# Attention and two mixtures on one core: order of the first loads, a conversion's low word, the pace of the conversion, and 14 unread products

## Chip, cores and metric

The kernel runs on one core of one Trainium2 chip. The metric is the time of one execution on the device in microseconds. [...]

## What is computed

```
# attention: q, k, v (4, 8, 576, 64) f32
rel = pos[:, None] - pos[None, :]
mask_local = (rel >= 0) & (rel < 32)                       # heads 0 to 3
mask_strided = (rel >= 0) & (pos[None, :] % 32 == pos[:, None] % 32)   # heads 4 to 7
attn = softmax(where(mask, q @ k.T / 8, -1e9))
x = (attn @ v) as (2304, 512)
# first mixture: w_a, w_b (512, 1536), w_out (1536, 512)
x = ((x @ w_a) * (x @ w_b)) @ w_out
# second mixture: noisy top 2 of 8 experts, w1 (8, 512, 1024), w2 (8, 1024, 512)
noisy = x @ w_gate + log1p(exp(x @ w_noise)) * noise
out[t] = sum over the two best e of softmax weight * (relu(x[t] @ w1[e]) @ w2[e])
```

The weights w_a, w_b and w_out arrive as float64; all else is float32.

## The kernel before

**Stages.** Four batches of 576 tokens go through attention in units of two heads (HPS = 0, 2, 1, 3: local and strided pairs in turn). The first mixture takes the tokens in five chunks c (512 tokens of each batch, then the four tails of 64 together) and twelve slices f of 128 hidden columns; ORDER lists the pairs (c, f). The attention of batch 0 runs alone at first; that of the batches 1 to 3 is cut into small steps (`att_pipe`, a generator) that run between the products of the first mixture. Then come the router, the scatter of tokens to experts, and the experts. The change lies in the first 150 us of about 1150.

**A unit of attention** (class `Unit`). `load_qk` and `load_v` issue its loads on SyncE. `T` transposes q and k on TensorE (L247) and ScalarE copies them out (L251). `Q` makes the scores sc (the mask as a product, L270, the scores, L279) and takes the maxima on VectorE (L283); for batch 1 ScalarE copies the scores to s (L289) and VectorE reduces (L303). `E` forms the exponentials on ScalarE (L307 or L312) and divides by the sums on VectorE: L314 adds, L315 inverts, L316 multiplies, into the softmax tile s. `P` transposes s on TensorE (L324), ScalarE copies (L325), and `PV` multiplies by v (L337), copies to xf (L340) and stores the last 64 tokens into tails on SyncE (L342). Two halves of a unit have a tile s each. `split_kd` splits a unit's result into a high and a low part (L403, L404).

**Products of three.** Every large product is done as three of fp32r (`mm3`, L184 to L188): high by high, high by low, low by high, 512 columns each. `stage_a` forms pa and pb from the chunk and the slices of w_a and w_b; ScalarE copies pa into a (L686), VectorE multiplies a by pb (L691), and a is split into gh and gl (L692, L693). `stage_b` multiplies by w_out into po.

**Conversion.** The float64 weights are loaded as pairs of 32-bit words (tile raw, low word L and high word Hw), one block per SyncE instruction (L158, `load_raw`), and `split64` (L161) makes a high and a low fp32r weight of each (w0h, w0l and so on) in two steps: VectorE masks the high word into m (tile ct, L167), ScalarE shifts its exponent (L168), VectorE adds the sign (L170), ScalarE writes the high part (L171); VectorE then cuts out the nine low bits of Hw (L173), joins the low word to them (L174), takes the exponent (L175) and writes the low part (L176). There are 24 blocks of two steps each, 48 steps: six of 512 columns (f = 0 and f = 1: w_a, w_b, w_out each), twelve of 1024 columns (two f each, f = 2 to 9), six of 512 columns (f = 10 and 11). Three raw buffers take turns; the load of a block waits until the block three before it is converted. `conv_to(n)` writes the code on up to step n: 12 steps (six blocks) along the attention of batch 0, and then, in chunk 0, by L778, four steps a slice f up to f = 5, and six a slice after that.

**Who sets the order.** TensorE's order is that of the code from the first mixture on (L773), SyncE's in the attention of batch 0 (L650). VectorE's and ScalarE's queues, and TensorE's in the first stage, are laid out by the scheduler when the kernel is built; on the chip each engine then takes its queue strictly in order. "Block 7" below is the seventh in the order of the slices: w_a of f = 2 and 3.

**Small loads.** `late_setup` (L105, called at L801) loads the gate weights wg and the noise in ten small loads (L106 to L112) and fills the table of the scatter. The setup (L71 to L103) makes the masks on VectorE and GpSimd; the tile ones, all 1.0, is written at L90. The first load of batch 0's q waits for the setup's last VectorE instruction.

Of the kernel before, what the change touches and what calls it, by code (L numbers as in the profile page):

```python
# [9 lines left out]
F32 = mybir.dt.float32  # L10
# [3 lines left out]
U32 = mybir.dt.uint32  # L14
AF = mybir.ActivationFunctionType
OP = mybir.AluOpType
# [16 lines left out]
def attention_moe_kernel(ctx: ExitStack, tc: tile.TileContext, q, k, v, w_a, w_b, w_out,  # L33
                         w_gate, w_noise, noise, w1, w2, out):
    nc = tc.nc
    B, H, S, D = q.shape
# [31 lines left out]
    wg = cpool.tile([128, KD, 16], F32, name="wg")  # L68
    noise_sb = cpool.tile([128, NTL, 8], F32, name="noise_sb")

    with tc.tile_pool(name="setup", bufs=1) as sp:  # L71
        rel = sp.tile([128, 128], I32, name="rel")
        nc.gpsimd.iota(rel, pattern=[[-1, 128]], base=0, channel_multiplier=1)
# [13 lines left out]
        nc.vector.tensor_scalar(r3f[:, 0], r3f[:, 0], 0.0, NEG, op0=OP.is_gt, op1=OP.mult)  # L87
        nc.vector.tensor_add(maskS, r3f[:, 0], r3f[:, 1])
        nc.vector.tensor_scalar(tri, relf, 0.0, None, op0=OP.is_lt)
        nc.vector.memset(ones, 1.0)  # L90
        nc.gpsimd.iota(iota8, pattern=[[1, 8]], base=0, channel_multiplier=0,
                       allow_small_or_imprecise_dtypes=True)
        nc.gpsimd.iota(base, pattern=[[NT, 8]], base=0, channel_multiplier=0,
# [8 lines left out]
            nc.gpsimd.iota(ids[TL * i:TL * i + TL, 4 * B:NTL], pattern=[[2 * S, 2]], base=S * i + CT,  # L102
                           channel_multiplier=1)  # L103

    def late_setup():  # L105
        nc.sync.dma_start(wg[:, :, 0:8], w_gate.rearrange("(k p) e -> p k e", p=128))  # L106
        nc.sync.dma_start(wg[:, :, 8:16], w_noise.rearrange("(k p) e -> p k e", p=128))
        for b in range(B):
            nc.sync.dma_start(noise_sb[:, 4 * b:4 * b + 4, :],
                              noise[S * b:S * b + CT, :].rearrange("(t p) e -> p t e", p=128))  # L110
            i = TL * (b % 2)
            nc.sync.dma_start(noise_sb[i:i + TL, 4 * B + b // 2, :], noise[S * b + CT:S * b + S, :])  # L112
        nrow = E * NT // 128
        fill = rpool.tile([128, nrow, 2], I32, name="fill", tag="x2T")
        nc.gpsimd.iota(fill[:, :, 0], pattern=[[1, nrow]], base=0, channel_multiplier=nrow)
        nc.vector.tensor_scalar(fill[:, :, 0], fill[:, :, 0], PAD - 1, None, op0=OP.bitwise_and)
        nc.vector.tensor_scalar(fill[:, :, 0], fill[:, :, 0], NT, None, op0=OP.add)
        nc.vector.memset(fill[:, :, 1], 0)
        nc.sync.dma_start(table.rearrange("(p r) c -> p r c", p=128), fill)
# [41 lines left out]
    def split64(raw, hi, lo):  # L161

        L, Hw = raw[:, :, 0], raw[:, :, 1]
        v = lambda a: a.rearrange("p (n m) -> p n m", n=hi.shape[1])
        m = conv_room["ct"](raw.shape[1])

        nc.vector.tensor_scalar(m, Hw, i32(0x7FFFFE00), None, op0=OP.bitwise_and)  # L167
        nc.scalar.activation(m.bitcast(U32), m, AF.Copy, scale=8.0, bias=-float(896 << 23))  # L168
        yield
        nc.vector.scalar_tensor_tensor(m, Hw, i32(0x80000000), m, op0=OP.bitwise_and, op1=OP.bitwise_or)  # L170
        nc.scalar.activation(hi, v(m.bitcast(F32)), AF.Copy)  # L171

        nc.vector.tensor_scalar(Hw, Hw, 0x1FF, None, op0=OP.bitwise_and)  # L173
        nc.vector.scalar_tensor_tensor(L.bitcast(F32), L.bitcast(U32), 2.0 ** -32, Hw, op0=OP.mult, op1=OP.add)  # L174
        nc.vector.tensor_scalar(Hw, m, i32(0xFF800000), None, op0=OP.bitwise_and)  # L175
        nc.vector.scalar_tensor_tensor(lo, v(L.bitcast(F32)), 2.0 ** -20, v(Hw.bitcast(F32)),  # L176
                                       op0=OP.mult, op1=OP.mult)
        yield

# [437 lines left out]
    nconv = [0]  # L617

    def conv_to(n):
        while nconv[0] < n:  # L620
            nconv[0] += 1
            next(conv)
# [23 lines left out]
    def bank1(name, shape):  # L646
        return pt(shape)

    us = [Unit(p1tile, bank0, 0, hp, "pe", (False, i > 0)) for i, hp in enumerate(HPS)]
    with tc.manual_schedule(engines={mybir.EngineType.SP}):  # L650
        for i, u in enumerate(us):
            u.load_qk()
            u.load_v()
            conv_room["ahead"](min(i + 1, 3))
        for i, _ in enumerate(att_pipe(us, 9, lambda u: split_kd(0, u.hp))):
            conv_to(min(12, i * 12 // 50))
        conv_to(12)
    a1.close()
    tp = m1.enter_context(tc.tile_pool(name="third", bufs=1, reuse_waits="tile"))
    last_units(tp, 8, ("w80", "w81", "w82"))  # L660

    def atile(name, shape):
        if name in ("ql", "kl"):
            return stage.tile(shape, F32, name=name, tag=f"st{int(name == 'kl')}")
        return apool.tile(shape, F32, name=name, tag=name, bufs=2 if name in ("s", "sst") else 1)

    us = [Unit(atile, bank1, b, hp, "act" if b == 1 else "dve", (b > 1,) * 2) for b in range(1, B) for hp in HPS]
    us[0].load_qk()
    us[0].load_v()
    attended = set()  # L670
    may = [1]
    attq.append(att_pipe(us, 1, lambda u: attended.add((u.b, u.hp)), lambda u: u.b <= may[0]))
# [100 lines left out]
    with tc.manual_schedule(engines={mybir.EngineType.PE}):  # L773
# [1 line left out]
        prev = None  # L775
        npt = [0]
        for c, f in ORDER:
            n0, n1 = nconv[0], min(48, 12 + 4 * (f + 1) if f < 6 else 36 + 6 * (f - 5))  # L778

            def point():  # L780
                npt[0] += 1
# [5 lines left out]
                if c == NCH - 1:  # L787
                    advance(bgq)

            if c == 0 and f == 6:  # L790
                conv_to(36)
                last_units(cp, 10, ("u0", "u1", "u2"))
                conv_room["raw"] = halves(rpool, [128, 512, 2], "raw", "row")
                conv_room["ct"] = lambda m: rpool.tile([128, 512], I32, name="ct", tag="x2T")
# [211 lines left out]
```

## Time and profile before

| | |
|---|---|
| median of 3 runs | 1155.91 us (1155.74 to 1158.33) |
| profiled execution | 1154.18 us, span 1152.4 us |
| TensorE busy | 1096.9 us, 95% of the span |
| VectorE busy | 523.1 us, 45% |
| ScalarE busy | 414.2 us, 36% |
| GpSimd busy | 142.0 us, 12% |
| granted clock of TensorE, mean | 0.986 |

The span is the time between the first and the last record of the profiled execution; the execution's own time is 1.8 us more. Busy time is the sum of an engine's records without overlap. The shares are averages over stages with different limits: in the first 40th of the span TensorE is busy 4 tenths, after the fourth 9 tenths or more nearly throughout. The page's own figures of the start are too coarse for this change, so the rows below come from views of single stretches.

### The profile page before, as it was taken

What the parts mean: (1) busy time and instruction counts of PE and PEld (TensorE: products, weight loads), DVE (VectorE), ACT (ScalarE), POOL (GpSimd) and SP (SyncE); (2) the same over time, 40 slices, a digit from 0 to 9 for tenths busy, and PEclk for the clock granted to TensorE, in tenths of its full rate; (3) what the DMA queues carried; (4) which work ended last, traced back from release to release, by engine and by line L of the source; (5) the groups of instructions that cost most, each with busy time, mean ns of one, the idle gap of its engine ahead of it and who ended that gap; (6) DMA issues with size and microseconds to landing.
All of it is one profiled execution on the core that took longest, in us unless ns stands there. A gap on an engine that the chain in (4) does not pass through costs nothing. (4 is left out here: it accounts for less than half of the span.)

```text
span 1152.4 us, 16080 instructions
## 1 busy us (share of the span) xinstructions
PE 1096.9 (95%) x6397; PEld 931.6 (81%) x6397; DVE 523.1 (45%) x1099; ACT 414.2 (36%) x911; POOL 142.0 (12%) x136
## 2 busy tenths in 40 slices
PE   4987999999999999999997999999999999999996
PEld 3766777788777877888887989998999899898995
DVE  4889876545446354223125452255343434342211
ACT  4666765333233232212124442244342423332110
POOL 0000000000200020002000314231021312121112
PEclk9998999999999999999999999999999999999998
DMA  9355433110112101730003443176354544442123
GB/s 193 87 190 174 142 109 82 38 59 11 37 32 56 49 16 49 262 122 1 1 37 92 133 142 54 42 173 187 105 115 123 124 114 117 121 115 43 19 28 49
DMA packets 88549, 105.02 MB, mean 91 GB/s; under 512 B 43664, under 2 KB 48400, under 8 KB 88464
## 3 DMA queue, kind: packets, MB, share of 16 engines
q1 hardware_dynamic: 78352, 82.89, 24.3%
q0 software_dynamic: 10112, 21.02, 10.1%
q8 instruction: 52, 0.85, 0.3%
q14 instruction: 33, 0.27, 0.1%
HBM read 78.53 MB, written 25.35 MB: 90 GB/s over the span
## 5 line engine op out<-in xcount | busy, mean ns | idle before, releaser
L856 DVE SCALAR_TENSOR_TENSOR hl<-ph,hh 128x256 fp32r<-128x256 f32 (+1 forms) x128 | 62.2, 489 | 212.2 <-ACT hh L855 211.8
L855 ACT ACTIVATE hh<-ph 128x256 fp32r<-128x256 f32 (+1 forms) x128 | 55.0, 433 | 222.9 <-PE ph L188 222.8
L691 DVE TENSOR_TENSOR a<-a,pb 128x512 f32<-128x512 f32 (+1 forms) x60 | 38.0, 633 | 129.8 <-PE pb L188 129.8
L499 POOL DMA_INDIRECT table<-pay,sli x36 | 35.5, 986 | 439.7 <-DVE sli L487 317.6
L880 POOL DMA_INDIRECT out_dram<-y,tb x40 | 64.0, 1600 | 183.7 <-ACT y L879 142.1
L686 ACT ACTIVATE a<-pa 128x512 f32<-128x512 f32 (+1 forms) x60 | 33.2, 553 | 136.8 <-PE pa L188 136.7
L692 ACT ACTIVATE gh<-a 128x512 fp32r<-128x512 f32 (+1 forms) x60 | 35.2, 587 | 84.4 <-DVE a L691 83.9
L746 POOL DMA_INDIRECT g<-x,tb x40 | 40.0, 999 | 191.2 <-PE tt L755 165.6
L693 DVE TENSOR_TENSOR gl<-a,gh 128x512 fp32r<-128x512 f32 (+1 forms) x60 | 38.0, 633 | 15.9 <-ACT gh L692 15.5
L324 PE MATMUL tt<-ident,s 72*72 72x72 f32 (+1 forms) x224 | 30.6, 268 | 9.1 <-DVE sst L314 6.2
L279 PEld LDWEIGHTS tt<-kT,qT 64*72 64x72 f32 (+1 forms) x336 | 29.5, 149 | 11.9 <-issue 9.8
L324 PEld LDWEIGHTS tt<-ident,s 72*72 72x72 f32 (+1 forms) x224 | 23.4, 144 | 18.9 <-issue 8.1
L279 PE MATMUL tt<-kT,qT 64*72 64x72 f32 (+1 forms) x336 | 37.6, 253 | 0.0
L325 ACT ACTIVATE pT<-tt 128x288 f32<-128x288 f32 (+1 forms) x64 | 25.0, 406 | 31.1 <-PE tt L324 31.0
L186 PE MATMUL py<-w6h,hh 128*128 128x512 f32 x80 | 32.2, 404 | 2.4 <-ACT hh L855 2.4
L186 PE MATMUL pa<-xh,w0h 128*128 128x512 f32 (+1 forms) x80 | 32.7, 409 | 1.5 <-ACT xh L403 1.5
L186 PE MATMUL pb<-xh,w1h 128*128 128x512 f32 (+1 forms) x80 | 33.0, 413 | 0.0
L187 PE MATMUL py<-w6l,hh 128*128 128x512 f32 x80 | 32.0, 400 | 0.0
L187 PE MATMUL pa<-xl,w0h 128*128 128x512 f32 (+1 forms) x80 | 31.1, 389 | 0.8 <-DVE xl L404 0.8
L186 PE MATMUL py<-w3h,hh 128*128 128x512 f32 x80 | 31.8, 398 | 0.0
L186 PE MATMUL py<-w2h,hh 128*128 128x512 f32 x80 | 31.8, 399 | 0.0
L186 PE MATMUL pa<-xh,w3h 128*128 128x512 f32 (+1 forms) x80 | 31.7, 396 | 0.0
(292 smaller groups left out, 3274.8 us busy)
## 6 DMA issues: line engine op xcount, KB each, us to landing
st<-in_moe_w_dram SPq DMA_DIRECT2D x64, 512.0 KB
out_dram<-zero SPq DMA_DIRECT2D x13, 512.0 KB
raw<-in_moe_w_out_dram SPq DMA_DIRECT2D x4, 1024.0 KB
raw<-in_moe_w_a_dram SPq DMA_DIRECT2D x4, 1024.0 KB
raw<-in_moe_w_b_dram SPq DMA_DIRECT2D x4, 1024.0 KB
x<-row SPq DMA_DIRECT2D x16, 256.0 KB
raw<-in_moe_w_a_dram SPq DMA_DIRECT2D x4, 512.0 KB
raw<-in_moe_w_b_dram SPq DMA_DIRECT2D x4, 512.0 KB
```

What stands on the lines that cost most here:

```text
L186: nc.tensor.matmul(ps, w[0], x[0], start=start, stop=False)
L187: nc.tensor.matmul(ps, w[0], x[1], start=False, stop=False)
L279: nc.tensor.matmul(ps[:, ii, :], self.qT[r0:r0 + 64, q0:q0 + n], self.kT[r0:r0 + 64, k0:k0 + m], start=not pemask, stop=not pemask or ii = ...
L324: nc.tensor.transpose(ps[:, ii, :], self.s[half][:, x, ii, :], ident[:n, :n])
L499: ins = nc.gpsimd.indirect_dma_start(out=table, out_offset=bass.IndirectOffsetOnAxis(ap=sli[:, 2 * j + kk:2 * j + kk + 1], axis=0), in_=pa ...
L691: nc.vector.tensor_mul(a, a, pb)
L692: nc.scalar.activation(gh, a, AF.Copy)
L693: nc.vector.tensor_sub(gl, a, gh.bitcast(F32))
L746: nc.gpsimd.indirect_dma_start(out=g, out_offset=None, in_=x2, in_offset=bass.IndirectOffsetOnAxis(ap=TB[e, t][:, 0:1], axis=0))
L855: nc.scalar.activation(hh, ph, AF.Relu)
L856: nc.vector.scalar_tensor_tensor(hl, ph, 0.0, hh.bitcast(F32), op0=OP.max, op1=OP.subtract)
L880: ins = nc.gpsimd.indirect_dma_start(out=out, out_offset=bass.IndirectOffsetOnAxis(ap=TB[e, t][:, 0:1], axis=0), in_=y, in_offset=None, co ...
```

## The change

The change has four parts. (1) The loads of batch 1's first unit, which the scheduler had put at the front of SyncE's queue, are written into the part of the code in which SyncE's order is fixed, behind those of batch 0; the ten small loads move out of `late_setup` into a function `late_load`, called at the end of that part. (2) In `split64` ScalarE takes the low word down by nine bits (new L179), and VectorE joins it to the shifted high word in one instruction (L184); the old cutting instruction L173 goes, and the last factor is another. (3) The conversion's pace in chunk 0 is three steps a slice up to f = 7 in place of four up to f = 5; the change of buffers moves from f = 6 to f = 8. (4) ones is written first of all, and 14 products of 128 x 512 of it go into a tile named idle that nothing reads.

New line numbers of the old ones: L158 is L168, L167 is L177, L168 is L178, L170 is L181, L171 is L182, L174 to L176 are L184 to L186, L218 is L228, L283 is L293, L285 is L295, L308 is L318, L310 is L320, L314 to L316 are L324 to L326, L342 is L352, L404 is L414, L691 to L693 are L702 to L704.

```diff
--- before.py
+++ after.py
@@ -67,6 +67,15 @@
     ids = cpool.tile([128, NTL], I32, name="ids")
     wg = cpool.tile([128, KD, 16], F32, name="wg")
     noise_sb = cpool.tile([128, NTL, 8], F32, name="noise_sb")
+
+    def warm(n):
+
+        ps = psum.tile([128, 4, 128], F32, name="idle", tag="A")
+        for _ in range(n):
+            nc.tensor.matmul(ps, ones, ones[:, None, :].to_broadcast([128, 4, 128]), start=True, stop=True)
+
+    nc.vector.memset(ones, 1.0)
+    warm(14)
 
     with tc.tile_pool(name="setup", bufs=1) as sp:
         rel = sp.tile([128, 128], I32, name="rel")
@@ -87,7 +96,6 @@
         nc.vector.tensor_scalar(r3f[:, 0], r3f[:, 0], 0.0, NEG, op0=OP.is_gt, op1=OP.mult)
         nc.vector.tensor_add(maskS, r3f[:, 0], r3f[:, 1])
         nc.vector.tensor_scalar(tri, relf, 0.0, None, op0=OP.is_lt)
-        nc.vector.memset(ones, 1.0)
         nc.gpsimd.iota(iota8, pattern=[[1, 8]], base=0, channel_multiplier=0,
                        allow_small_or_imprecise_dtypes=True)
         nc.gpsimd.iota(base, pattern=[[NT, 8]], base=0, channel_multiplier=0,
@@ -102,7 +110,7 @@
             nc.gpsimd.iota(ids[TL * i:TL * i + TL, 4 * B:NTL], pattern=[[2 * S, 2]], base=S * i + CT,
                            channel_multiplier=1)
 
-    def late_setup():
+    def late_load():
         nc.sync.dma_start(wg[:, :, 0:8], w_gate.rearrange("(k p) e -> p k e", p=128))
         nc.sync.dma_start(wg[:, :, 8:16], w_noise.rearrange("(k p) e -> p k e", p=128))
         for b in range(B):
@@ -110,6 +118,8 @@
                               noise[S * b:S * b + CT, :].rearrange("(t p) e -> p t e", p=128))
             i = TL * (b % 2)
             nc.sync.dma_start(noise_sb[i:i + TL, 4 * B + b // 2, :], noise[S * b + CT:S * b + S, :])
+
+    def late_setup():
         nrow = E * NT // 128
         fill = rpool.tile([128, nrow, 2], I32, name="fill", tag="x2T")
         nc.gpsimd.iota(fill[:, :, 0], pattern=[[1, nrow]], base=0, channel_multiplier=nrow)
@@ -166,14 +176,14 @@
 
         nc.vector.tensor_scalar(m, Hw, i32(0x7FFFFE00), None, op0=OP.bitwise_and)
         nc.scalar.activation(m.bitcast(U32), m, AF.Copy, scale=8.0, bias=-float(896 << 23))
+        nc.scalar.activation(L.bitcast(U32), L.bitcast(U32), AF.Copy, scale=2.0 ** -9, bias=-1.0)
         yield
         nc.vector.scalar_tensor_tensor(m, Hw, i32(0x80000000), m, op0=OP.bitwise_and, op1=OP.bitwise_or)
         nc.scalar.activation(hi, v(m.bitcast(F32)), AF.Copy)
 
-        nc.vector.tensor_scalar(Hw, Hw, 0x1FF, None, op0=OP.bitwise_and)
-        nc.vector.scalar_tensor_tensor(L.bitcast(F32), L.bitcast(U32), 2.0 ** -32, Hw, op0=OP.mult, op1=OP.add)
+        nc.vector.scalar_tensor_tensor(L, Hw, 23, L, op0=OP.logical_shift_left, op1=OP.bitwise_or)
         nc.vector.tensor_scalar(Hw, m, i32(0xFF800000), None, op0=OP.bitwise_and)
-        nc.vector.scalar_tensor_tensor(lo, v(L.bitcast(F32)), 2.0 ** -20, v(Hw.bitcast(F32)),
+        nc.vector.scalar_tensor_tensor(lo, v(L.bitcast(U32)), 2.0 ** -43, v(Hw.bitcast(F32)),
                                        op0=OP.mult, op1=OP.mult)
         yield
 
@@ -646,27 +656,28 @@
     def bank1(name, shape):
         return pt(shape)
 
+    def atile(name, shape):
+        if name in ("ql", "kl"):
+            return stage.tile(shape, F32, name=name, tag=f"st{int(name == 'kl')}")
+        return apool.tile(shape, F32, name=name, tag=name, bufs=2 if name in ("s", "sst") else 1)
+
     us = [Unit(p1tile, bank0, 0, hp, "pe", (False, i > 0)) for i, hp in enumerate(HPS)]
     with tc.manual_schedule(engines={mybir.EngineType.SP}):
         for i, u in enumerate(us):
             u.load_qk()
             u.load_v()
             conv_room["ahead"](min(i + 1, 3))
+        later = [Unit(atile, bank1, b, hp, "act" if b == 1 else "dve", (b > 1,) * 2) for b in range(1, B) for hp in HPS]
+        later[0].load_qk()
+        later[0].load_v()
         for i, _ in enumerate(att_pipe(us, 9, lambda u: split_kd(0, u.hp))):
             conv_to(min(12, i * 12 // 50))
         conv_to(12)
+        late_load()
+    us = later
     a1.close()
     tp = m1.enter_context(tc.tile_pool(name="third", bufs=1, reuse_waits="tile"))
     last_units(tp, 8, ("w80", "w81", "w82"))
-
-    def atile(name, shape):
-        if name in ("ql", "kl"):
-            return stage.tile(shape, F32, name=name, tag=f"st{int(name == 'kl')}")
-        return apool.tile(shape, F32, name=name, tag=name, bufs=2 if name in ("s", "sst") else 1)
-
-    us = [Unit(atile, bank1, b, hp, "act" if b == 1 else "dve", (b > 1,) * 2) for b in range(1, B) for hp in HPS]
-    us[0].load_qk()
-    us[0].load_v()
     attended = set()
     may = [1]
     attq.append(att_pipe(us, 1, lambda u: attended.add((u.b, u.hp)), lambda u: u.b <= may[0]))
@@ -775,7 +786,7 @@
         prev = None
         npt = [0]
         for c, f in ORDER:
-            n0, n1 = nconv[0], min(48, 12 + 4 * (f + 1) if f < 6 else 36 + 6 * (f - 5))
+            n0, n1 = nconv[0], min(48, 12 + 3 * (f + 1) if f < 8 else 36 + 6 * (f - 7))
 
             def point():
                 npt[0] += 1
@@ -787,7 +798,7 @@
                 if c == NCH - 1:
                     advance(bgq)
 
-            if c == 0 and f == 6:
+            if c == 0 and f == 8:
                 conv_to(36)
                 last_units(cp, 10, ("u0", "u1", "u2"))
                 conv_room["raw"] = halves(rpool, [128, 512, 2], "raw", "row")
```

**SyncE, the start.** The queue's first rows before; ql, kl and vl are batch 1's, qkv batch 0's (names with a number), raw a weight block.

```order
L218 DMA ql<-in_q_dram 96x6x64 x2
L218 DMA kl<-in_k_dram 96x6x64 x2
L226 DMA vl<-in_v_dram 128x2x64
L229 DMA vl<-in_v_dram 128x5x64 x2
L106 DMA wg<-in_moe_w_gate_dram 128x4x8
L218 DMA qkv_162<-in_q_dram 96x6x64 x2
L218 DMA qkv_162<-in_k_dram 96x6x64 x2
L226 DMA qkv_167<-in_v_dram 128x2x64
L229 DMA qkv_167<-in_v_dram 128x5x64 x2
```

The same engine after the change:

```order
L228 DMA qkv_177<-in_q_dram 96x6x64 x2
L228 DMA qkv_177<-in_k_dram 96x6x64 x2
L236 DMA qkv_182<-in_v_dram 128x2x64
L239 DMA qkv_182<-in_v_dram 128x5x64 x2
L168 DMA raw<-in_moe_w_a_dram 128x4x256
```

Batch 0's first unit now leads. Batch 1's four rows stand behind batch 0's last unit:

```order
L230 DMA qkv_199<-in_q_dram 72x2x512
L230 DMA qkv_205<-in_k_dram 72x2x512
L243 DMA qkv_205<-in_v_dram 72x2x512
L228 DMA ql<-in_q_dram 96x6x64 x2
L228 DMA kl<-in_k_dram 96x6x64 x2
L236 DMA vl<-in_v_dram 128x2x64
L239 DMA vl<-in_v_dram 128x5x64 x2
L168 DMA raw<-in_moe_w_a_dram 128x4x256
L352 DMA tails<-xf 128x64
```

**SyncE, the small loads.** After the change they stand together between the fourth store of tails and the w_out block of f = 4 and 5 (the twelfth block):

```order
L352 DMA tails<-xf 128x64
L114 DMA wg<-in_moe_w_gate_dram 128x4x8
L115 DMA wg<-in_moe_w_noise_dram 128x4x8
L117 DMA noise_sb<-in_moe_noise_dram 128x4x8
L120 DMA noise_sb<-in_moe_noise_dram 64x8
L117 DMA noise_sb<-in_moe_noise_dram 128x4x8
L120 DMA noise_sb<-in_moe_noise_dram 64x8
L117 DMA noise_sb<-in_moe_noise_dram 128x4x8
L120 DMA noise_sb<-in_moe_noise_dram 64x8
L117 DMA noise_sb<-in_moe_noise_dram 128x4x8
L120 DMA noise_sb<-in_moe_noise_dram 64x8
L168 DMA raw<-in_moe_w_out_dram 128x2x1024
```

Before, they stood between batch 0's last unit and the second weight slice's blocks:

```order
L220 DMA qkv_190<-in_k_dram 72x2x512
L233 DMA qkv_190<-in_v_dram 72x2x512
L107 DMA wg<-in_moe_w_noise_dram 128x4x8
L109 DMA noise_sb<-in_moe_noise_dram 128x4x8
L112 DMA noise_sb<-in_moe_noise_dram 64x8
L109 DMA noise_sb<-in_moe_noise_dram 128x4x8
L112 DMA noise_sb<-in_moe_noise_dram 64x8
L109 DMA noise_sb<-in_moe_noise_dram 128x4x8
L158 DMA raw<-in_moe_w_a_dram 128x4x256
L112 DMA noise_sb<-in_moe_noise_dram 64x8
L109 DMA noise_sb<-in_moe_noise_dram 128x4x8
```

What moved is the place of the ten rows, from ahead of the first store of tails to behind the fourth.

**VectorE, block 7.** With numbers of the tiles: raw_563 is block 7 before, raw_588 after; raw_663 is block 8 and raw_796 block 9, a w_out block that SyncE loads ahead of block 7; sst_643 and s_642 before, sst_669 and s_668 after, are the fourth unit's softmax. Before:

```order
L404 TENSOR_TENSOR xl_522<-xf_449,xh_521 128x512
L315 RECIPROCAL sst_600<-sst_600 72x8
L308 TENSOR_REDUCE sst_643<-s_642 72x8
L316 TENSOR_TENSOR s_599<-s_599,sst_600 72x576
L314 TENSOR_SCALAR sst_643<-sst_643 72x8
L167 TENSOR_SCALAR ct_240<-raw_563 128x1024
L315 RECIPROCAL sst_643<-sst_643 72x8
L316 TENSOR_TENSOR s_642<-s_642,sst_643 72x576
L170 SCALAR_TENSOR_TENSOR ct_240<-raw_563,ct_240 128x1024
L167 TENSOR_SCALAR ct_240<-raw_638 128x1024
```

After:

```order
L184 SCALAR_TENSOR_TENSOR raw_796<-raw_796 128x1024
L295 TENSOR_TENSOR s_668<-sc_670,sst_669 72x288
L293 TENSOR_REDUCE sst_669<-sc_691 72x4
L295 TENSOR_TENSOR s_668<-sc_691,sst_669 72x288
L177 TENSOR_SCALAR ct_265<-raw_588 128x1024
L324 TENSOR_SCALAR sst_625<-sst_625 72x8
L325 RECIPROCAL sst_625<-sst_625 72x8
L326 TENSOR_TENSOR s_624<-s_624,sst_625 72x576
L184 SCALAR_TENSOR_TENSOR raw_588<-raw_588 128x1024
L318 TENSOR_REDUCE sst_669<-s_668 72x8
L177 TENSOR_SCALAR ct_265<-raw_663 128x1024
```

The fourth unit's sums stood ahead of block 7 and stand behind it now, and a joining instruction of block 9 stands ahead of it.

**VectorE, up to s.** The tile s that ends here is that of the first half of batch 1's first unit. Before:

```order
L173 TENSOR_SCALAR raw<-raw 128x1024
L176 SCALAR_TENSOR_TENSOR w4l<-raw 128x4x256
L167 TENSOR_SCALAR ct<-raw 128x1024
L310 TENSOR_SCALAR sst<-sst 96x6
L174 SCALAR_TENSOR_TENSOR raw<-raw 128x1024
L314 TENSOR_SCALAR sst<-sst 96x6
L170 SCALAR_TENSOR_TENSOR ct<-raw,ct 128x1024
L175 TENSOR_SCALAR raw<-ct 128x1024
L315 RECIPROCAL sst<-sst 96x6
L173 TENSOR_SCALAR raw<-raw 128x1024
L176 SCALAR_TENSOR_TENSOR w5l<-raw 128x1024
L316 TENSOR_TENSOR s<-s,sst 96x768
```

After:

```order
L704 TENSOR_TENSOR gl<-a,gh 128x512
L184 SCALAR_TENSOR_TENSOR raw<-raw 128x1024
L185 TENSOR_SCALAR raw<-ct 128x1024
L186 SCALAR_TENSOR_TENSOR w3l<-raw 128x4x256
L177 TENSOR_SCALAR ct<-raw 128x1024
L320 TENSOR_SCALAR sst<-sst 96x6
L186 SCALAR_TENSOR_TENSOR w4l<-raw 128x4x256
L324 TENSOR_SCALAR sst<-sst 96x6
L181 SCALAR_TENSOR_TENSOR ct<-raw,ct 128x1024
L325 RECIPROCAL sst<-sst 96x6
L185 TENSOR_SCALAR raw<-ct 128x1024
L326 TENSOR_TENSOR s<-s,sst 96x768
```

Between block 7's first instruction and this s there were 48 rows, the two included, and are 60. The blocks whose instructions stand ahead of s reach further: a second pair of blocks for the tiles w3l and w4l has been converted there, and a first mask instruction of the next.

## Rows read from the trace of the kernel before

**Rows 1.** Waits of TensorE, 0 to 130 us: total, times, longest in us.

```profile
PE sc L247 <- DMA qkv<-in_q_dram: 10.8, 1, 10.8
PE tt L324 <- DVE sst L314: 6.2, 1, 6.2
```

**Rows 2.** Waits of TensorE, 130 to 1152 us.

```profile
PE tt L474 <- DVE ms L467: 6.9, 1, 6.9
```

**Rows 3.** Timeline of TensorE: start and duration in us, form, count, idle before.

```profile
81.57 1.16 PE L247 MATMUL tt<-ident,ql 96*128 96x96 f32 x6
...
83.44 0.63 PE L188 MATMUL pb<-xh,w1l 128*128 128x512 f32 x1
83.86 0.63 PE L186 MATMUL pb<-xh,w1h 128*128 128x512 f32 x1
...
87.62 0.39 PE L188 MATMUL pa<-xh,w0l 128*128 128x512 f32 x1
87.85 0.40 PE L186 MATMUL pa<-xh,w0h 128*128 128x512 f32 x1
...
103.22 0.40 PE L188 MATMUL pa<-xh,w0l 128*128 128x512 f32 x1
109.86 1.19 PE L324 MATMUL tt<-ident,s 96*128 96x96 f32 x6 [6.25 <-DVE sst L314]
```

**Rows 4.** Windows: busy us (instructions) by engine, granted clock, DMA share, GB/s.

```profile
83.01:85.14 2.13, 2.13 (x6) 1.65 (x5) 2.10 (x3) 1.45 (x3) 0.00 (x0) 1.00 0.89 302
...
110.76:115.20 4.44, 4.44 (x13) 3.47 (x13) 4.44 (x7) 2.44 (x4) 0.00 (x0) 0.50 0.51 207
```

**Rows 5.** Timeline of VectorE: setup, sixth and seventh block, softmax tile s.

```profile
0.85 0.17 DVE L90 MEMSET ones<- 128x128 bf16 x1 [0.85 <-PEq L990]
...
4.84 0.29 DVE L81 TENSOR_TENSOR maskAB<-tmp 96x128 bf16<-96x128 f32 x1
...
56.13 0.69 DVE L176 SCALAR_TENSOR_TENSOR w2l<-raw 128x512 fp32r<-128x512 f32 x1
...
66.03 0.69 DVE L167 TENSOR_SCALAR ct<-raw 128x1024 int32<-128x1024 int32 x1 [0.70 <-DMA raw<-in_moe_w_a_dram]
...
108.77 0.94 DVE L316 TENSOR_TENSOR s<-s,sst 96x768 f32<-96x768 f32 x1
109.64 0.16 DVE L314 TENSOR_SCALAR sst<-sst 96x6 f32<-96x6 f32 x1
```

**Rows 6.** Windows: start to sixth block's end; seventh block to s. Columns of rows 4.

```profile
16.29:56.82 40.53, 33.93 (x213) 25.57 (x211) 32.56 (x76) 25.68 (x90) 0.00 (x0) 1.00 0.59 127
66.03:109.64 43.61, 33.33 (x178) 24.51 (x176) 41.52 (x54) 30.42 (x63) 0.00 (x0) 0.96 0.50 159
```

**Rows 7.** Timeline of SyncE's DMA issues, first 130 us.

```profile
0.76 1.40 SPq L218 DMA_DIRECT2D ql<-in_q_dram  x2
...
5.97 1.25 SPq L218 DMA_DIRECT2D qkv<-in_q_dram  x2
...
27.43 0.51 SPq L109 DMA_DIRECT2D noise_sb<-in_moe_noise_dram  x1
...
60.23 0.34 SPq L342 DMA_DIRECT2D tails<-xf  x1
60.63 0.43 SPq L158 DMA_DIRECT2D raw<-in_moe_w_a_dram  x1
...
78.30 0.34 SPq L342 DMA_DIRECT2D tails<-xf  x1
```

**Rows 8.** VectorE's groups by form, 0 to 140 us: busy us, mean ns, idle before.

```profile
L170 DVE SCALAR_TENSOR_TENSOR ct<-raw,ct 128x1024 int32<-128x1024 int32 x11 | 13.4, 1221 | 1.9 <-ACT ct L168 1.8
...
L167 DVE TENSOR_SCALAR ct<-raw 128x1024 int32<-128x1024 int32 x12 | 8.3, 688 | 0.8 <-DMA raw<-in_moe_w_a_dram 0.7
...
L316 DVE TENSOR_TENSOR s<-s,sst 72x576 f32<-72x576 f32 x5 | 3.7, 749 | 0.1
```

**Rows 9.** ScalarE's groups by form, 0 to 140 us. Columns of rows 8.

```profile
L168 ACT ACTIVATE ct<-ct 128x1024 uint32<-128x1024 int32 x12 | 12.8, 1066 | 4.3 <-DVE ct L167 4.3
```

## Prediction

> **What bounds the kernel now.** I first read who waited for whom on TensorE. In the first 130 us [rows 1] it has two waits of over 6 us: 10.8 us for the first q at the very start, and 6.2 us for VectorE. From 130 us on its longest wait, 6.9 us [rows 2], is the router's for ms, in a stage that the change doesn't touch. So the kernel is a stream of products behind a start of some 110 us, and what the change is worth is the time by which TensorE leaves that start earlier or later.
>
> TensorE's timeline [rows 3] shows the place where it leaves: at 109.86 us, with the transposes of the first softmax tile s of batch 1. It stood from 103.45 us (0.23 us after the start of its last product) until VectorE had finished that s. [...]
>
> VectorE's timeline [rows 5] and windows [rows 6] tell why s was late. From 66.03 us, when the seventh weight block had landed, to 109.64 us, the end of s, VectorE was busy 41.5 of 43.6 us. It works strictly in the order of its queue, and s (108.77) stands behind conversions. From 16.29 to 56.82 us (the end of the sixth block) it was busy only 32.6 of 40.5 us: there it waits for data. So the exit from the start is set by two things: when block 7 lands, and how much work the queue holds from there to s.
>
> **The change part by part.** My sums start from the profiled execution (span 1152.4, 1154.18 us in all). The median of the runs shown, 1155.91, is 1.7 us more; I add the shift to the median.
>
> *First batch first.* SyncE [rows 7] issued batch 1's first loads from 0.76 us and batch 0's first q at 5.97. Now q is first, but it still waits for the last setup instruction on VectorE, which ends at 4.84 + 0.29 = 5.13 us [rows 5]. Issue is 0.8 us earlier, and the queue ahead of it is empty; the first transposes, which now start behind the 10.8 us wait, come 0.8 us earlier, or 2.4 if the 4.8 us from that issue to the end of the wait also shrink by a third with nothing ahead; I take 1. Beyond that little is won: batch 1's loads move from the front of the queue to behind the fourth unit's, but there they ran while SyncE waited for the setup, so the later blocks land about when they did. Batch 1's q is first used at 81.57 us [rows 3] and is covered.
>
> *14 products.* They can start at 0.85 + 0.17 = 1.02 us, when the ones are written [rows 5]. At 0.43 us each they end at 7.0 us. TensorE waits for q until 8.4 us or later, so they cost nothing; if their cover went (q at 5), it would be 2 us.
>
> *Conversion.* A block of 1024 columns takes three two-operand instructions (1.22 us) and three one-operand ones (0.69 us) on VectorE [rows 8]. One of the latter goes: 0.69 us off VectorE per block. ScalarE gets one more ACTIVATE, 1.07 us by its sibling L168 [rows 9]. Over the 12 large blocks that is 8.3 us off VectorE and 12.8 us onto ScalarE; the 12 half blocks (f = 0, 1, 10, 11) do about half of this again.
>
> *The order.* The new pace (3 steps a unit instead of 4) acts on the order in which the code is written, but VectorE's and ScalarE's queues are laid out by the scheduler, and the printed order shows what became of it: conversions come forward, not back. From block 7's first instruction to s the new queue has 60 rows where the old had 48. Counted by kind: eight two-operand instructions of 1024 columns more (L181 three, L184 two, L186 three); one one-operand one fewer (six L173 removed, two L177 and three L185 added); and five of softmaxes, which stood ahead of the stretch before: a multiplication and a reduction over 576 columns and three tiny ones. Priced start to start (an instruction starts some 0.07 us before the record of the last one ends: 108.77 + 0.94 against 109.64 [rows 5]): 8 x 1.15 = 9.2, minus 0.62; 2 x 0.68 [rows 8] and 3 x 0.1 (0.16 each [rows 5]) for the softmaxes, 1.7. Sum: **10.2 us more work between block 7 and s.** A shift of the ninth block (raw_796, a w_out block that is loaded ahead of block 7) now stands before it; ScalarE's pass for that, 1.07 us, has the time until block 7 lands, so I cost it at nothing.
>
> *When block 7 lands.* It was issued at 60.63 us, 3.8 us after the sixth block was converted and 0.4 us after the second unit's tails store, which stands ahead of it on SyncE [rows 7]; VectorE took it up at 66.03, 5.4 us after the issue. Now block 6 is converted earlier. Latest: all waits stay, the start is 1 us earlier, and six half instructions are gone (6 x 0.35 = 2.1): 53.7. Earliest: half of the 8.0 us of waiting [rows 6] goes too: 49.7. From there to the issue 0.4 to 3.8 us, to the landing 5.4: between 55.5 and 62.9. I take 58.9, near the middle: the tails store needs TensorE and ScalarE, and the first of these is faster now. That is 7.1 us earlier than 66.0.
>
> *Sum.* 10.2 - 7.1 = 3.1; the 2.1 us that VectorE stood idle in the old stretch [rows 6] I let stand. **s is ready, and TensorE leaves the start, 3.1 us later.** Bounds: 10.2 - 10.5 - 2.1 = -2.4, and 10.2 - 3.1 = +7.1. [...] Behind it the products are the same and the queue's lead only grows, so nothing of the 3.1 us comes back: 1155.91 + 3.1 = **1159.0 us**.
>
> **Rivals.**
> [...]
> - *The ten small loads block the twelfth block (slower).* The gate and noise loads have moved: they stood between the loads of batch 0, and now stand between the fourth tails store and block 12, 0.5 us of issue each [rows 7], more when they wait for earlier transfers. Block 12 can then be issued only at some 83 to 87 us (fourth tails store at 77 to 78, where it was [rows 7], plus 5.5 to 9) and lands 5.4 us later; VectorE comes to it at about 59 + 27 = 86 us, 27 us being what its queue holds from block 7 to there at these prices, and the product a<-a,pb stands right behind. From a landing later than 86 us it decides: at 90, 4 us more, 1163 us.
> - *ScalarE becomes the bound (slower).* It was busy 30.4 of 43.6 us [rows 6]. In the new stretch it gets nine of the new passes (9.6 us), four more conversions (4.2) and exps of the fourth unit (about 4): 48 us of records, in 51. If its in-order waits for blocks push exps back, s is 2 to 4 us later still: 1162 us. [...]
> - *The pace does nothing.* The scheduler pulls the conversions forward whatever the pace; this is part of the forecast already.
>
> **How the numbers follow.** Less than about 0.3% (3.5 us) can't be told from no change here. The forecast gets 0.48, the faster start 0.24, the late small loads 0.15, ScalarE 0.13. The forecast's own spread, -2.4 to +7.1, lies for about five sixths within 3.5 us: 0.40 same and 0.08 slower. So faster 0.24, same 0.40, slower 0.08 + 0.15 + 0.13 = 0.36. The range goes from 1149 (the faster start) to 1164 (the upper bound of the sum, 1163, and the small loads).
>
> **What would show it.** Right: VectorE's queue from block 7's landing (57 to 61 us) to s takes some 53 us with few gaps, s ends at 111 to 115 us, and TensorE's one long wait is still that for s, and longer than 6.2 us. The 14 products are done before the first q lands. [...]

## The result and the profile after

The changed kernel takes 1162.74 us (median of 6, 1157.61 to 1164.78) against 1155.83 (median of 6, 1152.98 to 1158.33) for the kernel before. The ratio is 1.0057, with an interval of 1.0040 to 1.0075: 6.6 us slower, 4.6 to 8.7. The profiled execution, 1157.61 us with a span of 1155.8, is the shortest of the six; against the profiled one of before it is 3.4 us longer.

Waits of TensorE after the change, 0 to 130 us:

```profile
PE tt L334 <- DVE s L326: 6.4, 2, 5.3
PE tt L347 <- ACT pT L335: 3.7, 2, 3.3
PE pa L196 <- ACT xh L413: 3.5, 1, 3.5
PE sc L257 <- DMA qkv<-in_q_dram: 3.0, 1, 3.0
```

The wait for s is still the longest, and at the same place. It is 5.3 us and not 6.2, although s is later, because TensorE itself arrives later: its transposes of s begin at 113.18 us, so it stands from 107.86 us, before from 103.61 [rows 3].

```profile
113.18 1.19 PE L334 MATMUL tt<-ident,s 96*128 96x96 f32 x6 [5.32 <-DVE s L326]
```

VectorE's timeline after the change at block 7, the twelfth block and s:

```profile
60.85 0.69 DVE L177 TENSOR_SCALAR ct<-raw 128x1024 int32<-128x1024 int32 x1
...
89.71 0.69 DVE L177 TENSOR_SCALAR ct<-raw 128x1024 int32<-128x1024 int32 x1 [2.51 <-DMA raw<-in_moe_w_out_dram]
...
112.09 0.95 DVE L326 TENSOR_TENSOR s<-s,sst 96x768 f32<-96x768 f32 x1
```

Block 7 is taken up 5.2 us earlier than before [rows 5] and s starts 3.3 us later. The window from block 7 to the end of s (columns of [rows 4]) shows why:

```profile
60.85:113.04 52.19, 36.47 (x191) 26.63 (x190) 48.91 (x65) 43.14 (x80) 0.00 (x0) 0.73 0.60 178
```

VectorE is busy 48.9 of 52.2 us, before 41.5 of 43.6 [rows 6]: 7.4 us more work and 1.2 us more idle time, less 5.2 us by which the stretch begins earlier, is 3.4. To follow TensorE further I use ScalarE's copies of pa; the eighteenth is the last one ahead of the next stall, and starts 0.49 us after its product's last instruction does (at 286.47 us before, at 289.53 after). ScalarE's timeline, of the kernel before, then of the one after:

```profile
286.96 0.60 ACT L686 ACTIVATE a<-pa 128x512 f32<-128x512 f32 x1 [2.17 <-PE pa L188]
```

```profile
290.02 0.60 ACT L697 ACTIVATE a<-pa 128x512 f32<-128x512 f32 x1 [2.17 <-PE pa L198]
```

It is 3.1 us late: what was lost at s stands unchanged 177 us later. The stall behind it is the scatter's. VectorE's timeline near 300 us, before and after:

```profile
299.83 0.24 DVE L490 COPY pay<-ids 128x4 int32<-128x4 int32 x2 [3.05 <-DMA table<-pay,sli]
```

```profile
305.07 0.24 DVE L500 COPY pay<-ids 128x4 int32<-128x4 int32 x2 [5.23 <-DMA table<-pay,sli]
305.22 0.95 DVE L316 TENSOR_TENSOR s<-s,sst 96x768 f32<-96x768 f32 x1
```

The tile pay holds the token numbers that are scattered into the table. The scheduler has put a copy into pay, which has two buffers, ahead of a softmax; VectorE waits at it until a scatter has landed, 3.05 and 5.23 us. TensorE's timeline there, before and after (the wait is put down to ScalarE's qT, which stands behind that softmax in ScalarE's queue):

```profile
302.64 0.47 PE L324 MATMUL tt<-ident,s 96*128 96x96 f32 x3 [0.85 <-ACT qT L251]
```

```profile
307.88 0.47 PE L334 MATMUL tt<-ident,s 96*128 96x96 f32 x3 [3.02 <-ACT qT L261]
```

The code there is the same, and the changed kernel loses another 2.2 us, of which 1.8 are gone again by the span's end. The forecast had not looked at this place.

### The profile page after: what moved, and what is told of

Same layout as the page of the kernel before. It is cut to its first block, busy times and chain, and to the rows that moved or that the text cites. A ratio compares the mean times of both kernels' runs of the same rounds, so it can differ in the third digit from the quotient of the medians.

```text
span 1155.8 us, 16107 instructions
## 1 busy us (share of the span) xinstructions
PE 1100.2 (95%) x6411; PEld 932.1 (81%) x6411; DVE 512.4 (44%) x1075; ACT 432.8 (37%) x935; POOL 142.3 (12%) x136
## 4 chain that ended last, share of the span: by engine, by line
PE 79%; DMA 7%; DVE 5%; ACT 4%; issue 2%; POOL 1%; SPq 1%; DVEq 0%; ACTq 0%; POOLq 0%
PE ph L197 6%; PE ph L196 6%; PE ph L198 6%; PE py L196 6%; PE py L197 6%; PE py L198 6%; PE po L196 4%; PE pb L196 4%; PE pa L196 4%; PE po L198 4%; PE po L197 4%; PE pb L197 3%; PE pb L198 3%; PE pa L197 3%; PE pa L198 3%; PE tt L289 3%
## 5 line engine op out<-in xcount | busy, mean ns | idle before, releaser
L702 DVE TENSOR_TENSOR a<-a,pb 128x512 f32<-128x512 f32 (+1 forms) x60 | 37.9, 632 | 133.1 <-PE pb L198 133.1
L704 DVE TENSOR_TENSOR gl<-a,gh 128x512 fp32r<-128x512 f32 (+1 forms) x60 | 38.1, 634 | 17.0 <-ACT gh L703 16.5
```

The lines of the kernel that those rows point to most:

```text
L702: nc.vector.tensor_mul(a, a, pb)
L704: nc.vector.tensor_sub(gl, a, gh.bitcast(F32))
```

## The experiments

Each set of four shares a chip and the runs of the kernel before on it; the sets are on different chips, so ratios are compared within a set first. Beside the time stand the start of s (VectorE) and the eighteenth copy of pa (ScalarE), from each profile. Block 7 stands for its first instruction on VectorE.

| | edit | block 7 | s | 18th pa | span | median, ratio to before |
|---|---|---|---|---|---|---|
| before | | 66.03 | 108.77 | 286.96 | 1152.4 | |
| after | | 60.85 | 112.09 | 290.02 | 1155.8 | 1162.74, 1.0057 |
| e1 | old conversion | 63.19 | 103.40 | 282.8 | 1153.1 | 1154.81, 0.9994 |
| e2 | no products | 60.97 | 110.60 | 288.6 | 1158.7 | 1160.33, 1.0045 |
| e3 | small loads back | 62.29 | 111.43 | 289.6 | 1161.0 | 1161.49, 1.0044 |
| e4 | blocks 13 on behind s | 61.21 | 102.02 | 283.5 | 1154.8 | 1156.15, 1.0007 |
| e5 | before, five pay | 67.77 | 109.92 | 287.7 | 1154.0 | 1155.19, 1.0002 |
| e6 | after, five pay | 62.15 | 113.35 | 292.5 | 1158.8 | 1160.17, 1.0054 |
| e7 | e1, five pay | 61.70 | 101.72 | 278.6 | 1144.0 | 1146.14, 0.9931 |
| e8 | before, new conversion, five pay | 70.87 | 113.22 | 289.7 | 1156.2 | 1158.00, 1.0031 |
| e9 | e4, five pay | 60.65 | 100.74 | 279.0 | 1149.1 | 1151.43, 0.9983 |
| e10 | e7, no products | 64.16 | 104.87 | 282.3 | 1149.1 | 1150.91, 0.9982 |
| e11 | e7, old pace | 60.90 | 100.82 | 277.4 | 1147.7 | 1150.63, 0.9984 |
| e12 | e7, blocks 12 on behind s | 61.81 | 97.41 | 274.2 | 1140.6 | 1146.02, 0.9945 |

In eleven of the fourteen profiles TensorE waits for s (3.0 to 7.7 us), and there the eighteenth copy stands 176.5 to 179.4 us behind the start of s, while s itself differs by 12.5 us: the start of s decides TensorE's progress. In e4, e9 and e12 it doesn't wait for this s; what decides there is when TensorE arrives at its transposes (109.22, 104.75 and 99.11 us).

**e1, the old conversion.** From the changed kernel:

```diff
-        nc.scalar.activation(L.bitcast(U32), L.bitcast(U32), AF.Copy, scale=2.0 ** -9, bias=-1.0)
...
-        nc.vector.scalar_tensor_tensor(L, Hw, 23, L, op0=OP.logical_shift_left, op1=OP.bitwise_or)
+        nc.vector.tensor_scalar(Hw, Hw, 0x1FF, None, op0=OP.bitwise_and)
+        nc.vector.scalar_tensor_tensor(L.bitcast(F32), L.bitcast(U32), 2.0 ** -32, Hw, op0=OP.mult, op1=OP.add)
...
```

The last factor goes back with them.

> The changed kernel with the old conversion (the cutting instruction back on VectorE, ScalarE's new pass gone). Theory 'exit': the end is the moment at which the first softmax tile s of batch 1 is ready, plus a constant: in the two traces s is ready at 109.64 and 112.96 us and the spans are 1152.4 and 1155.8, so 1042.8 us lie behind it in both. VectorE's queue from block 7 to s has 54 rows here, as before the change, and w5l is not yet in it; priced as in the prediction 37.7 us (before 39.7, which took 43.6; after 46.4, which took 52.1). With block 7 taken up at 61 to 65 us, s at 103 to 108, span 1146 to 1151, time 1148 to 1153. Rival 'loads': the new order of the loads and the late small ones are the cause and the conversion is not; then the time stays at 1158 to 1164, and TensorE still waits over 5 us for s. Rival 'ScalarE': the new pass on ScalarE is the cost; then it also falls, but with s ready where the queue price says later than 108.

Ratio 0.9994 (0.9978 to 1.0011): the loss is gone, with s 8.7 us earlier than in the changed kernel. VectorE has more instructions per block again, and s comes earlier all the same; so what counts at s is how much conversion stands ahead of it in the queue (54 instructions from block 7 to s, 63 in the changed kernel), not the cost of one block. Theory "exit" gave 1148 to 1153 and misses by 1.8 us; the profile shows where the rest went, TensorE's timeline near 300 us:

```profile
301.93 0.74 PE L334 MATMUL tt<-ident,s 96*128 96x96 f32 x3 [4.27 <-ACT qT L261]
```

TensorE stands 4.3 us at the scatter's stall, where the kernel before stood 0.85.

**e2, no products.**

```diff
-    warm(14)
```

> The changed kernel without the 14 unread products. Theory 'exit': the products end before q lands and cost and give nothing themselves; the queue from block 7 to s has 61 rows instead of 63 (44.6 us for 46.4), so s 0 to 2 us earlier and the time 0 to 2 us below the changed kernel: 1159 to 1163. [...]

Ratio 1.0045 (1.0027 to 1.0063), s 1.5 us earlier: as the queue's price said. Without the products the kernel isn't slower (1.0045 for the changed kernel's 1.0057, not to be told apart).

**e3, the small loads back.**

```diff
-        late_load()
...
+                late_load()
                 late_setup()
```

> The changed kernel with the ten small loads called where they were, so that the scheduler places them. Theory 'exit': VectorE's wait for the twelfth block (2.5 us at 87.2 us in the changed kernel's trace) goes or shrinks; the queue up to s has 65 rows, 47.1 us for 46.4; s 1 to 2.5 us earlier, time 1159 to 1162. Rival: the wait for that block is due to its raw buffer or to the DMA engines, not to the place of the small loads; then the wait stays over 2 us and the time within 1 us.

VectorE's 2.5 us wait for the twelfth block is gone (no wait for a load in its list from 60 to 112 us), but s starts only 0.7 us earlier (block 7 itself is taken up 1.4 us later), and the ratio, 1.0044 (1.0025 to 1.0062), isn't told from the changed kernel's. The rival of the small loads was real on VectorE, and small at s.

**e4, s ahead of later conversions.** Behind the multiplication that makes s, every conversion instruction from step 25 on is queued by an order edge (the scheduler must lay it behind that multiplication). The conversion's instructions stand under `with behind():`.

```diff
+    def behind():
+        return tc.issue_after(gate[0].ins) if gate and nconv[0] >= 25 else ExitStack()
...
+        with behind():
...
-            nc.vector.tensor_mul(s3, s3, over(sm))
+            mul = nc.vector.tensor_mul(s3, s3, over(sm))
+            if self.b == 1 and self.hp == 0 and half == 0:
+                gate.append(mul)
```

> The changed kernel with the conversion of blocks 13 and later put behind s in VectorE's queue (an order edge, no wait). The queue from block 7 to s falls from 63 rows (46.4 us) to 46 (32.8). Theory 'exit': s is ready at about 99 us, before TensorE's products ahead of it are done (at 107 us), so the 5.3 us wait goes and with it the stretch at 0.50 behind it (4.4 us of it, worth 2.2): 6 to 9 us less than the changed kernel, 1152 to 1157. Rival 'moved wait': TensorE waits at the next place instead (the second half of s, or w3 to w5), and gives back most: within 2 us of the changed kernel.

Ratio 1.0007 (0.9990 to 1.0025), in the range of theory "exit". All instructions of the changed kernel run; only their order differs, and 5 to 6 us come back. s is 10.1 us earlier, and the eighteenth copy only 6.5: TensorE begins its transposes of s at 109.22 us without a wait, 6.2 us after s is done, so more than the 5.3 us of the wait and the slow stretch behind it (in the changed kernel the granted clock is 0.50 from 113.20 to 117.60 us) was not to be had at this place. The second half of s now comes 19 us behind the first (121.14 us); TensorE waits 0.9 us for it.

**e5 to e8, five buffers of pay.**

```diff
-        pay = rpool.tile([128, J, 2, 2], I32, name="pay", tag="pay", bufs=2)
+        pay = rpool.tile([128, J, 2, 2], I32, name="pay", tag="pay", bufs=5)
```

e5 is the kernel before with it, e6 the changed one, e7 is e1 with it, e8 is e5 with the new conversion alone.

> The kernel before with five buffers of pay instead of two, so that VectorE writes all token numbers in the setup and no longer waits for the scatter near 300 us (3.0 us there, TensorE 0.8 us behind it; in the changed kernel 5.2 and 3.0 us). Theory 'scatter': the waits of VectorE for the scatter (13.8 us in three waits, before) reach TensorE two or three times and are what lies between the 3.0 us by which the changed kernel's profile is late at 287 us and the 6.6 us of the medians; without them the time falls by 1 to 4 us to 1151 to 1154. Rival: they are covered; within 1 us of before.

> The changed kernel with five buffers of pay. Theory 'scatter': 3 to 7 us less than the changed kernel (1154 to 1158), and the distance to the kernel before with five buffers is that of the start alone, 3 us (2 to 4). Rival 'start': all of the 6.6 us come from the start, and the distance stays at 6 to 7 us.

> The changed kernel with the old conversion and five buffers of pay. In the profile of the old conversion TensorE's progress at 283 us was 4.2 us ahead of the kernel before, and the time was the same: theory 'scatter' says that the scatter took it, so here 4 us below the kernel before with five buffers, 1147 to 1150, under both kernels. Rival: the gain is lost elsewhere; within 1 us of the kernel before with five buffers.

> The kernel before with five buffers of pay and the new conversion alone (old loads, old pace, no products). VectorE's queue from block 7 to s has 52 rows, 39.5 us, against 54 rows and 39.7 us. Theory 'queue' (what counts is the conversion work that the scheduler puts ahead of s, not the new instructions themselves): s within 2 us of that of the kernel before, time within 2 us of the kernel before with five buffers. Rival 'ScalarE': the new pass itself costs; 4 to 7 us more.

The wait for the scatter is gone in all four, and behind the eighteenth copy all four have 865.4 to 866.5 us to the span's end. For the kernel before this gives nothing that can be measured (1.0002, 0.9983 to 1.0020: "scatter" misses here), nor for the changed one (1.0054, 1.0035 to 1.0074). So the scatter doesn't explain the 6.6 us: between e5 and e6 lie 5.0 us by the medians, 4.8 by the spans and by the eighteenth copy, and 3.4 by s; 5.0 lies between the two expectations (2 to 4 and 6 to 7). In e7 the gain of the start reaches the end: 0.9931 (0.9908 to 0.9953), 9 us below e5 and better than expected (1146.14 us for 1147 to 1150). The same windows as above, e6, then e7:

```profile
62.15:114.30 52.15, 37.42 (x191) 27.36 (x190) 48.90 (x65) 43.29 (x80) 0.00 (x0) 0.70 0.57 177
```

```profile
61.70:102.67 40.97, 32.59 (x177) 23.86 (x175) 39.87 (x56) 27.71 (x53) 0.00 (x0) 0.78 0.58 175
```

Block 7 comes at the same time; with the new conversion VectorE has 9.0 us more to do ahead of s, with less work per block. The scheduler lays it out so: with the new conversion the second blocks of w3l and w4l (f = 6 and 7) are complete ahead of s (63 rows), with the old one the queue ends at the first block of w4l (f = 4 and 5; 55 rows). e8 shows another cost: alone, the new conversion makes 2.8 us by the medians (1.0031 against 1.0002, each plus or minus 0.2%, so hardly told from nothing); the median misses both expectations (within 2 us, and 4 to 7). There the stretch from block 7 to s is as long as in e5 (42.3 us to 42.1), but block 7 comes 3.1 us later. ScalarE's windows from 8 to 67 us (fourth busy column) are 33.2 us in e5, and in e8:

```profile
8.00:67.00 59.00, 46.19 (x280) 34.32 (x280) 37.52 (x82) 36.51 (x121) 0.00 (x0) 1.00 0.59 138
```

ScalarE does the six new passes in the first stage (0.68 to 0.71 us each) in line with the exponentials, and the stage as a whole is later. That the passes are the cause of this is the likeliest reading; no run takes them alone. The parts don't add up: by the medians of this set the new conversion alone costs 2.8 us, the rest of the change alone gains 9.1, and both together lose 5.0. The 11 us of difference lie in how they act together: from block 7 to the end of s VectorE is busy 41.6 us in e5, 41.3 in e8 and 39.9 in e7, but 48.9 in e6.

**e9 to e12.** e9 is e6 with the edit of e4; e10 is e7 without the products; e11 is e7 with the old pace; e12 is e7 with the edit of e4 from step 23 on.

> The changed kernel (new conversion) with blocks 13 and later behind s in VectorE's queue, and five buffers of pay. Queue from block 7 to s 46 rows, 32.8 us, against 63 rows and 46.4 us in the changed kernel with five buffers. Theory 'queue': the 14 us between the new and the old conversion (1160.2 and 1146.1 with five buffers) are the conversion work that the scheduler puts ahead of s; with that work behind s, s at 101 to 104 us and the time 1147 to 1152. Rival 'ScalarE': the new passes delay the exponentials whatever the order; s after 108 us and the time over 1155.

> The old conversion, the new loads and pace, five buffers of pay, without the 14 products. Queue 50 rows, 35.2 us, against 55 rows, 37.8 us, with them. Theory 'queue': the products change the time only by the order that the scheduler makes: s 0 to 3 us earlier, time 1143 to 1147. [...]

> The old conversion, the new loads, the products, five buffers of pay, and the old pace (four steps a slice). VectorE's queue up to s is the same, 55 rows, 37.8 us. Theory 'queue': the pace does nothing up to s; the time is 1145 to 1148, so the 9 us between this and the kernel before with five buffers belong to the order of the loads. Rival 'pace': the slower pace gives part of the 9 us; then 1149 or more.

> The old conversion, the new loads, pace and products, five buffers of pay, and blocks 12 and later behind s in VectorE's queue: 48 rows, 33.0 us, against 55 rows and 37.8 us. TensorE waits for s 3.0 us in the run without this edge. Theory 'queue': s up to 4 us earlier, of which TensorE can use the 3.0 us, and the stretch at 0.50 behind the wait goes: 1142 to 1146. Rival 'moved wait': the second s or the blocks that are now late make up for it: 1146 to 1149.

e9, ratio 0.9983 (0.9968 to 0.9998), is as "queue" said: with the new conversion on ScalarE, but later blocks behind s, s starts at 100.74 and the kernel is no slower than before. Rival "ScalarE" is out as the cause of the loss. It isn't out as a smaller cost: e9 and e12 are of one set, in neither does TensorE wait for s, and they differ in the conversion (and in one block at the order edge); e9 is 5.4 us slower. TensorE's timelines, of e9, then of e12:

```profile
104.75 0.66 PE L341 MATMUL tt<-ident,s 96*128 96x96 f32 x6
```

```profile
99.11 0.66 PE L341 MATMUL tt<-ident,s 96*128 96x96 f32 x6
```

With the new conversion TensorE comes to the transposes of s 5.6 us later, though it doesn't wait for s. No run shows which of its earlier waits makes this. e12, 0.9945 (0.9925 to 0.9965), starts s 4.3 us earlier than e7 and TensorE doesn't wait for it any more; e7 and e12 are both faster than both kernels, and the two can't be told apart; the median of e12, 1146.02, is the border of its two expectations. e10, 0.9982 (0.9967 to 0.9996), misses: without the products s is 3.2 us later than in e7, with block 7 at 64.16 for 61.70, not earlier, and the median is 1150.91 us, above the expected 1143 to 1147. A faster TensorE in e7 isn't seen: in e7 as in e10 the 512-column products start 0.43 us apart until 79.9 us, though few stand there before 78 us. The order, which the scheduler makes anew, is the likeliest cause, and not shown.

e11, 0.9984 (0.9968 to 1.0000), has the same start as e7 (s 0.9 us earlier): the pace does nothing up to s. But its median, 1150.63, is above the expected 1145 to 1148 and is what rival "pace" named (1149 or more). Behind the eighteenth copy its profile has 870.3 us, e9's 870.1, but those of e10 and e12 have 866.8 and 866.4, and e7's 865.4. Of the 4.9 us between e11 and e7, 1.4 come before the fiftieth copy of pa (near 593 us), where all four kernels of this set lose 1.4 to 2.1; the other 3.5 come behind it, while the last weight block is taken up at 173 us. So the pace has no direct part in them, but what makes them stays open.

## Why the prediction was right or wrong

*The bound.* Right: the exit from the start decides, and the loss stays; 3.3 us at s are 3.1 us at the eighteenth copy. What it left out is that TensorE itself comes to that place 4.2 us later (107.86 us for 103.61), so that an earlier s alone can win no more than the wait.

*First batch first.* The first transposes begin at 9.67 us for 10.75: 1.1 us earlier, 1 forecast. What I called little is much: with the old conversion the new loads, the pace and the products bring 9 us (e7 against e5). At s, e10 (loads and pace) is 5.1 us ahead of e5, and e7 (the products too) another 3.2. How much of it stays to the end without the new pace is open: e11's ratio is 0.9984.

*The order: the term that was mis-sized.* I counted 48 rows against 60 between block 7 and s, and the section on the change says the same. That took the ends of the stretch from two prints, of which one groups repeats. In one print there are 54 rows before and 63 after: L181, L184 and L186 two each more, not three, two and three; seven L173 removed, two L177 and three L185 added; five of softmaxes. At the same prices 6 x 1.15 - 2 x 0.62 + 1.7 = 7.4 us instead of 10.2; VectorE was busy 7.4 us longer.

*Block 7.* 5.2 us earlier, 7.1 forecast, inside the bounds (3.1 to 10.5). The two errors went opposite ways: forecast 10.2 - 7.1 = 3.1, measured 7.4 - 5.2 + 1.2 = 3.4. The 1.2 us are idle time of VectorE, which the sum let stand as it was; the wait for the twelfth block alone is 2.5 us. The right sum at s is partly luck. The choice of 58.9 us leaned on a faster TensorE ahead of the second unit's tails store. That store is issued at 55.16 us for 60.23, but no run shows a faster TensorE to be the cause: it is issued at 56.45 in e6, where the granted clock is 0.50 from 10 to 80 us, and at 56.53 in e10, which has no products.

*The median.* The forecast of 1159.0 fits the profiled execution (3.4 us) and is 3.7 us below the median. Of that the five-buffer pair explains some: there the start is worth 4.8 us, with the same code. The profile of the changed kernel was its shortest run, and I had no spread of it. What the other runs lose is not shown. By the prediction's own mark of 0.3% the 0.57% are slower, to which it gave 0.36, and not the same, to which it gave 0.40.

*Rivals.* The late small loads cost VectorE 2.5 us and s 0.7; in the time no difference can be told (e3: 1.0044 against 1.0057). ScalarE did not become the bound: 43.1 busy of 52.2 us beside VectorE's 48.9. The new pass measures 1.18 us for 1.07 assumed, ScalarE's group over 140 us:

```profile
L179 ACT ACTIVATE raw<-raw 128x1024 uint32<-128x1024 uint32 x12 | 14.1, 1178 | 9.5 <-DMA raw<-in_moe_w_out_dram 4.5 <-DMA raw<-in_moe_w_b_dram 2.7 <-DVE sst L293 1.2
```

It replaces 0.69 us on VectorE [rows 8]. The faster start, the range's 1149 us, no run of the changed kernel shows (the shortest is 1157.61). With the old conversion and five buffers of pay it came (e7, 1146.14 us), and the new conversion hid it; the clock isn't seen to bring it: in e7 the granted clock is 0.50 from 10 to 80 us.

*The signs.* Held: block 7 at 60.85 us (57 to 61), s done at 113.04 (111 to 115), the products done at 6.6 us (0.40 us each for 0.43), before the first q. One went the other way: TensorE's wait for s is 5.3 us, not longer than 6.2. Three more readings differ from the kernel before. VectorE's longest wait in the stretch is for a raw w_out block (2.5 us), as with late small loads. Products of 512 columns stand 0.23 us apart at 41.5 us, in the kernel before still 0.43 at 83.44 [rows 3]. The scatter's wait behind 130 us, 0.85 us before, is 3.0. By e3 and e6 neither the small loads nor the scatter carries the loss, and e6 has it with a granted clock of 0.50 from 10 to 80 us.

## What to carry to other kernels

A queue that a scheduler fills is part of the change. VectorE ran its queue as laid out: in both traces the twelve rows printed up to s start in the printed order (99.93 to 108.77 us before, 104.54 to 112.09 after). Here the new order put two more blocks ahead of the one instruction that the critical engine waited for, though each block was 0.69 us cheaper on VectorE, and the kernel got slower. It takes the parts together: with the cheaper block alone (e8) VectorE has no more work there. Count what stands ahead of that instruction in one and the same listing, and tie later work behind it (e4: the ratio falls from 1.0057 to 1.0007; e9 against e6: from 1.0054 to 0.9983) before making the work cheaper. Look for stalls behind the change too: at a two-buffer tile e1 lost its gain some 195 us behind s.

## What was unexpected of the hardware

Two values of the granted clock, a share of full speed, go with two paces: where it reads 0.50 behind the wait for s, products of 512 columns start 0.43 us apart (115.08 and 115.51 us in the changed kernel), and where it reads 1.00, 0.23 us apart (41.50 and 41.73). But the row reads 1.00 from the start in kernels without the products, though the 512-column products are 0.43 us apart (before, at 83.44 us; e2, at 83.88 us), and 0.50 from 10 us in the changed kernel, e6 and e7, which have them: the record seems to begin with the first change, so mean clocks of the two kinds (0.986 and 0.957) can't be compared. In the changed kernel's profile, and not in those of e6 and e7, TensorE had a granted clock of 1.00 from 36.7 us. TensorE's timeline and windows there:

```profile
36.87 0.42 PE L334 MATMUL tt<-ident,s 72*72 72x72 f32 x4
...
41.50 0.40 PE L197 MATMUL pa<-xl,w0h 128*128 128x512 f32 x1
41.73 0.39 PE L198 MATMUL pa<-xh,w0l 128*128 128x512 f32 x1
45.46 0.99 PE L347 MATMUL tt<-pT,qkv 72*64 72x72 f32 x12 [3.33 <-ACT pT L335]
```

```profile
33.00:36.60 3.60, 3.60 (x27) 3.23 (x27) 2.54 (x7) 3.60 (x18) 0.00 (x0) 0.50 0.91 167
36.70:42.00 5.30, 5.10 (x45) 3.60 (x43) 3.72 (x9) 3.53 (x8) 0.00 (x0) 1.00 0.87 263
45.50:58.00 12.50, 11.97 (x92) 9.05 (x92) 10.76 (x24) 8.99 (x27) 0.00 (x0) 0.50 0.36 105
```

The granted clock rose in a stretch in which TensorE was busy (3.60 of 3.60 us), stayed at 1.00 through eight transposes of s (two groups of four, at 36.87 and 39.39 us) that were mixed with other products, and was back at 0.50 by the end of the 3.3 us wait.
